# S loaded twice over on ScalarE's queue and turned by VectorE, in an attention and FFN kernel on one core

## The chip, the cores and the metric

The kernel runs on one core of a Trainium2 chip. The metric is the device time of one execution in microseconds (us), given as the median over several runs. The engines are TensorE (PE in the profile, with PEld for its weight loads), VectorE (DVE), ScalarE (ACT), GpSimd (POOL) and SyncE (SP); SP and ACT each have a queue on which they issue DMA transfers.

## The reference

Attention by a polynomial sketch, without a softmax, followed by a feed-forward layer (FFN) with a squared ReLU. There are 4 batches of 4 heads, 1088 positions and 32 dims per head; the sketches S1 and S2 are 8 x 32 each. The FFN has 4352 tokens, width 128 and 2048 hidden units.

```python
def phi(x):
    a = np.einsum('rd,bhsd->bhsr', S1, x)
    b = np.einsum('rd,bhsd->bhsr', S2, x)
    return np.einsum('bhsi,bhsj->bhsij', a, b).reshape(*x.shape[:-1], r * r)
q_p, k_p = (phi(q), phi(k))
kv = np.einsum('bhsf,bhsd->bhfd', k_p, v)
z = np.sum(k_p, axis=2)
num = np.einsum('bhsf,bhfd->bhsd', q_p, kv)
den = np.einsum('bhsf,bhf->bhs', q_p, z)[..., None] + 1e-06
x = ...      # num / den, heads side by side, 4352 x 128
h = np.maximum(x @ w_in, 0.0)
out = h * h @ w_out
```

## The kernel before

All of it is float32, with the first FFN matmul in a packed form of it. The tokens of the FFN are cut into ten chunks of 256 to 512 columns (`FC`). For each chunk and each of 16 blocks of 128 hidden units, TensorE multiplies `xT` by a block of `w_in` (L583, "pg"), ScalarE takes the ReLU (L592, "gt"), ScalarE or VectorE squares it (L600, L602, "g"), and TensorE multiplies by a block of `w_o` into an accumulator (L621, "po").

The attention of the batches is computed between those pieces. A planner, `_Order`, places them by costs and due times that are written into the code, and writes one fixed order for every engine. The change doesn't touch the planner's part. It touches the stretch before it, the first 14 us, where the order is the order of the program: the attention of batch 0, of which the first 256 queries are computed in one piece so that the FFN can start.

That stretch runs as follows. S1 is loaded by ACT's queue and S2 by SP's queue into `s_nat`, 8 rows each (L217, L218). On SP's queue there follow k of batch 0 in two parts, the first 256 columns of q, eight transfers of v, then in turn two quarters of `w_in`, a quarter of `w_o`, columns 256 to 640 of q, and the remaining weights. TensorE meanwhile runs five dummy matmuls (`keep_warm(W0)`, L672, 512 columns of bfloat16 ones, into "warm"). It then multiplies `s_nat` by a selection matrix `sel` (L683, four matmuls into "sp"). `sel` is built from an identity by VectorE's memset and two GpSimd copies (L230, L249, L252). ScalarE copies the result to `ss` (L686), 128 partitions by 80 columns: the first 64 columns, `sf`, hold the transposed S of each head in a block of its own, zeros elsewhere; the last 16, `s_T`, hold the transposed S1 and S2 in every head's 32 partitions. Four more dummies follow (`keep_warm(W1)`).

VectorE transposes k into `kt0` in three pieces (`a_kT0`, L283) and the first q into `qT` (L289). TensorE computes k's features, nine tiles of 128 positions (`a_kf`, L308, "kf", against `sf`), and ScalarE copies half of them to `kb` (L314). VectorE multiplies them to the 64 products `kp` (`a_kp0`, L324). TensorE sums them against v into "kvp" (`a_kv0`, L384). In between it computes both sketches of the first queries (`q0`, L734, tile "x", against `sq`, which GpSimd makes from `s_T` at L699). From "kvp" VectorE makes block matrices `bd` (L766) and `zm`, TensorE the denominator and numerator (L789), and VectorE the first 256 columns of `xT` (L812). With these the FFN starts (L583). `a_qc` (L296) computes the sketches of the second chunk of queries, from the transposed columns 256 to 640 of q.

On GpSimd the order is: memsets, the identity `iden`, the two `sel` copies, `sq`, then `irep` (four copies, L706), memsets, two copies of `s_T` into `sw` (L713), `sfk` (L714), memsets, and then the four casts of `w_in` (`cast_wi`, L665).

Of the kernel before, what the change touches and what calls it, by code (L numbers as in the profile page):

```python
# [9 lines left out]
F32 = mybir.dt.float32  # L10
# [4 lines left out]
def _ap(t: bass.AP, p0: int, np_: int, off: int, free):  # L15
    p = list(t.ap)[0]
    return bass.AP(
        t.tensor, t.offset + p0 * p[0] + off, [[p[0], np_]] + [list(d) for d in free]
    )
# [85 lines left out]
def kernel(  # L105
# [11 lines left out]
    nc = tc.nc  # L117

    B, H, S, D = 4, 4, 1088, 32
# [3 lines left out]
    E = 2  # L123
    NB = 16
    GT, G2, LA = 4, 6, 3.5
    LU = 4
    W0, W1, W3 = 5, 4, 1
    ND, QT, WI, KL, QL = 2, 3.0, (1.0, 1.9), (30.0, 12.0), 4.0


# [21 lines left out]
    psf = ctx.enter_context(tc.tile_pool(name="psf", bufs=2, space=bass.MemoryType.PSUM))  # L152
# [3 lines left out]
    def sb(name, cols, dt=F32, rows=128):  # L156
        return cpool.tile([rows, cols], dt, tag=name, name=name)
# [7 lines left out]
    kT, qT = sb("kT", SP), sb("qT", SP)  # L165
    xT = sb("xT", B * S + SP - S, F32R)
    w_in32, w_o, w_in = sb("w_in32", 2048), sb("w_o", 2048), sb("w_in", 2048, F32R)
    s_nat, ss, s2f = sb("s_nat", 32, rows=16), sb("ss", 80), sb("s2f", 32)
    sf, s_T = ss[:, 0:64], ss[:, 64:80]

    sw = [sb(f"sw{i}", 32) for i in range(2)]
    sfk = sb("sfk", 32)
# [3 lines left out]
    def load_k(eng, b, c0=0, c1=S):  # L176
        eng.dma_start(
            kn[b % 2][:, c0:c1],
            bass.AP(k.tensor, k.offset + b * H * S * D + c0, [[G * D, 128], [1, c1 - c0]]),
        )  # L180

    def load_q(eng, b, c0, c1):
        eng.dma_start(
            qn[b % 2][:, c0:c1],
            bass.AP(q.tensor, q.offset + b * H * S * D + c0, [[G * D, 128], [1, c1 - c0]]),
        )
# [16 lines left out]
    def load_wi(eng, c):  # L203
        eng.dma_start(
            w_in32[:, 512 * c : 512 * c + 512], moe_w_in[:, 512 * c : 512 * c + 512]
        )
# [7 lines left out]
            ),  # L214
        )

    nc.scalar.dma_start(s_nat[0:8, :], S1[:, :])  # L217
    nc.sync.dma_start(s_nat[8:16, :], S2[:, :])  # L218
    load_k(nc.sync, 0, 0, 512)
    load_k(nc.sync, 0, 512, S)  # L220
    load_q(nc.sync, 0, 0, 256)
# [4 lines left out]
    zero_a = sb("zero_a", 8)  # L226
    nc.scalar.copy(zero_a[:, :], nc.const_aps.tensor(0.0, (128, 8), F32))

    sq, sel = sb("sq", 256), sb("sel", 320, rows=16)
    nc.vector.memset(sel[:, :], 0.0)  # L230
    nc.gpsimd.memset(_ap(vn[0], 96, 32, 32 * (NT - 2), [[32 * NT, H], [1, 64]]), 0.0)
    nc.gpsimd.memset(vn[0][:, VC : VC + 32], 1.0)
    ones = vn[0][:, VC : VC + 32]
# [8 lines left out]
    for i in range(2):  # L242
        nc.vector.memset(own_p[64 * i : 64 * i + 64, i : i + 1], 1.0)
    iden, irep = sb("iden", 128), sb("irep", 128)
# [1 line left out]

    own_f, zm = sb("own_f", 16), sb("zm", 32)
    own_h, own_q = sb("own_h", 4), sb("own_q", 2)
    nc.gpsimd.tensor_copy(  # L249
        _ap(sel, 0, 16, 0, [[88, 4], [32, 2], [1, 8]]), _ap(iden, 0, 16, 0, [[0, 4], [8, 2], [1, 8]])  # L250
    )
    nc.gpsimd.tensor_copy(  # L252
        _ap(sel, 0, 16, 64, [[80, 4], [1, 16]]), _ap(iden, 0, 16, 0, [[0, 4], [1, 16]])
    )
    nc.vector.tensor_reduce(
        out=own_h[:, :], in_=_ap(iden, 0, 128, 0, [[32, 4], [1, 32]]), op=add, axis=AX
    )
# [22 lines left out]
    def a_kT0(t0, n):  # L280
        p = 3 if t0 + n > NT - 2 else 4
        i = 32 * (first(0, t0, 1) - first(0, t0, 0))
        nc.vector.transpose(  # L283
            _ap(kt0, 0, 128, 128 * t0, [[32, p], [128, n], [1, 32]]),
            _ap(kn[0], 0, 128, 32 * first(0, t0, 0), [[i, p], [32, n], [1, 32]]),
        )
# [16 lines left out]
    def a_kf(t0, n, pool, tag):  # L303
        kf = pool.tile([128, 512], F32, tag=tag, name="kf")
        for t in range(n):
            for c in range(4):
                o = 128 * (t0 + t) + 32 * c
                nc.tensor.matmul(  # L308
                    _ap(kf, 32 * c, 32, 32 * t, [[32 * n, 2], [1, 32]]),
                    kt0[:, o : o + 32],  # L310
                    sf,
                )
        kb = wpool.tile([128, 32 * 3], F32, tag="kb", bufs=4, name="kb")
        nc.scalar.copy(kb[:, 0 : 32 * n], kf[:, 32 * n : 64 * n])  # L314
        st["kf", t0] = kf, kb
# [137 lines left out]
    def a_w(b):  # L453
        pw = wpool.tile([128, 64], F32, tag="pw", bufs=1, name="pw")
        nc.vector.tensor_tensor(
            out=pw[:, :],
            in0=_ap(st[b, "kvp"], 0, 128, 32, [[64, E], [8, 4], [1, 8]]),
            in1=_ap(ss, 0, 128, 72, [[0, E], [0, 4], [1, 8]]),
            op=mult,
        )  # L460
        nc.vector.tensor_reduce(
            out=sw[b % 2][:, 16:24], in_=_ap(pw, 0, 128, 0, [[8, 8], [1, 8]]), op=add, axis=AX
        )
# [205 lines left out]
    def keep_warm(n, cols=512):  # L669
        t_ = st["warm"]  # L670
        for _ in range(n):
            nc.tensor.matmul(  # L672
                t_[:, 0:cols],
                nc.const_aps.tensor(1.0, (128, 128), mybir.dt.bfloat16),
                nc.const_aps.tensor(1.0, (128, cols), mybir.dt.bfloat16),
            )
# [1 line left out]

    st["warm"] = psf.tile([128, 512], F32, tag="pg", name="warm")
    keep_warm(W0)  # L680
    sp = psf.tile([128, 512], F32, tag="po", name="sp")
    for h in range(H):
        nc.tensor.matmul(  # L683
            sp[32 * h : 32 * h + 32, 0:80], s_nat[:, :], sel[:, 80 * h : 80 * h + 80]
        )
    nc.scalar.copy(ss[:, :], sp[:, 0:80])  # L686
    load_wi(nc.sync, 0)
    load_wi(nc.sync, 1)
    load_wo(nc.sync, 0)
# [3 lines left out]
    for c in range(1, 4):  # L693
        load_wo(nc.sync, c)
    load_q(nc.sync, 0, 640, S)
    keep_warm(W1)
    a_kT0(0, 4)
    for x in range(2):
        nc.gpsimd.tensor_tensor(  # L699
            out=_ap(sq, 0, 128, 128 * x, [[64, 2], [8, 8], [1, 8]]),  # L700
            in0=_ap(ss, 0, 128, 72 - 8 * x, [[0, 2]] + [[[0, 8], [1, 8]], [[1, 8], [0, 8]]][x]),
            in1=_ap(own_q, 0, 128, 0, [[1, 2], [0, 8], [0, 8]]),
            op=mult,
        )
    for h in range(H):
        nc.gpsimd.tensor_copy(  # L706
            _ap(irep, 32 * h, 32, 0, [[32, 4], [1, 32]]),
            _ap(iden, 32 * h, 32, 32 * h, [[0, 4], [1, 32]]),
        )
    nc.gpsimd.memset(_ap(vn[1], 96, 32, 32 * (NT - 2), [[32 * NT, H], [1, 64]]), 0.0)  # L710
    for w in sw:
        nc.gpsimd.memset(w[:, 16:32], 0.0)
        nc.gpsimd.tensor_copy(w[:, 0:16], s_T)  # L713
    nc.gpsimd.tensor_tensor(  # L714
        out=_ap(sfk, 0, 128, 0, [[16, 2], [1, 16]]),
        in0=_ap(ss, 0, 128, 64, [[0, 2], [1, 16]]),
        in1=_ap(own_q, 0, 128, 0, [[1, 2], [0, 16]]),
        op=mult,
    )
# [17 lines left out]
    qb0 = wpool.tile([128, 512], F32, tag="qb0", bufs=1, name="qb0")  # L737
    qp0 = wpool.tile([128, 512], F32, tag="qp0", bufs=1, name="qp0")
    a_kf(0, 2, psf, "po")
    a_kf(2, 2, psf, "pg")  # L740
    a_kf(4, 3, psf, "po")
    a_kf(7, 2, psf, "pg")
    q0(0)
# [3 lines left out]
    for t0, n in ((0, 2), (2, 2), (4, 3), (7, 2)):  # L747
# [5 lines left out]
        out=_ap(qp0, 0, 128, 0, [[256, 2], [1, 256]]), in0=banks(x0, 2, 0, 256),  # L753
        in1=_ap(qb0, 0, 128, 0, [[256, 2], [1, 256]]), op=mult,
    )
    nc.vector.transpose(s2f[:, :], _ap(ss, 0, 128, 72, [[0, 4], [1, 8]]))
    den0 = psf.tile([128, 512], F32, tag="po", name="den0")
    for y in range(2):
        nc.tensor.matmul(  # L759
# [13 lines left out]
    for c in range(4):  # L773
# [4 lines left out]
        in0=_ap(st[0, "kvp"], 0, 128, 32, [[64, 2], [0, 2], [1, 8]]),  # L778
        in1=_ap(own_f, 0, 128, 0, [[0, 2], [8, 2], [1, 8]]),
# [173 lines left out]
    def kv_tasks(b, k0):  # L953
        O.add(
            ("kvs", b), {"PE": 1.6}, k0, [("vn", b), ("ks", b, 3)], on(a_kvs, b),
            uses=[("kp", b, h) for h in range(H)], rings=[("att", 1)], lag=PEL,
        )
        O.add(
            ("w", b), {"DVE": 0.3}, k0 + 0.9, [], on(a_w, b), uses=[("kvs", b)],
        )  # L960
        O.add(
            ("kvt", b), {"DVE": 0.2}, k0 + 1.0, [("kvr", b - 1, 3)], on(a_kvt, b),
            uses=[("kvs", b)],
        )
        w = [("nd", b - 2, i) for i, _ in AC[b - 2]] if b > 1 else []
        for h in range(H):
            O.add(
                ("kvr", b, h), {"POOL": 0.95}, k0 + 2.0 + 0.1 * h, w + [("kvt", b)],
                on(a_kvr, b, h),
            )  # L970
# [21 lines left out]
    for u in range(NU):  # L992
        ci, c0, n, d0, m = units[u]
        w = n * m
# [37 lines left out]
        if d0 + m == NB and ci != last:  # L1032
            po = [x for u_ in range(first_unit[c0], u + 1) for x in pe2[u_]]
# [49 lines left out]
```

## Time and profile before

| | |
|---|---|
| median of 3 runs | 187.0 us (186.67, 187.0, 187.8) |
| the profiled execution | 187.0 us, of which the profile's span is 185.0 us |
| mean granted TensorE clock | 0.999 |
| PE busy | 180.1 us, 97% of the span |
| PEld busy | 104.4 us, 56% |
| ACT busy | 135.0 us, 73% |
| DVE busy | 120.1 us, 65% |
| POOL busy | 35.2 us, 19% |
| DMA | 11.25 MB, mean 61 GB/s |

The span runs from the first to the last instruction of the program; what lies around it is the difference to the execution's time. A busy time is the union of an engine's instructions, so that two that overlap count once. In a timeline line the first number is the start in us, the second the length of the merged group, then the engine, the line of the kernel, the operation, the tiles (written tile, arrow, read tiles) and the count; the bracket gives the idle time before the group and what ended it. A matmul on float32 stands as two records. DMA issues stand under SPq or ACTq, the time being that of the issue and not of the transfer.

### The profile page before, as it was taken

To read this page: it belongs to the slowest core of one execution; us is meant where nothing else is said; L and a number is where in the kernel's file an instruction comes from. 1 tells how busy PE (TensorE), PEld (TensorE's weight loads), DVE (VectorE), ACT (ScalarE), POOL (GpSimd) and SP (SyncE) were. 2 spreads that over 40 slices of the span, in tenths; PEclk is the share of its full clock that TensorE was granted. 3 is DMA by queue.
4 is the path that set the end of the run, shared out by engine and by line. 5 is a ranking of instruction groups with operands and counts; after the bars stand their busy time and mean duration, and the time that the engine had idled before them with its cause. 6 is when DMAs were issued, how large, how long until landed. Compare 5 with 4: busy or idle time off the path is not lost.

```text
span 185.0 us, 3893 instructions
## 1 busy us (share of the span) xinstructions
PE 180.1 (97%) x1478; PEld 104.4 (56%) x1478; DVE 120.1 (65%) x254; ACT 135.0 (73%) x262; POOL 35.2 (19%) x157
## 2 busy tenths in 40 slices
PE   8999999999999999999999999999999999999992
PEld 2757766666555566555454445545545555555791
DVE  4968969968994598699437984998243334222420
ACT  3319977769968887699585975795788878777760
POOL 4425405328400000870000003820000000000000
PEclk9999999999999999999999999999999999999999
DMA  4799700100038700000592100002103000300211
GB/s 160 186 334 330 177 4 2 25 7 4 0 50 226 181 0 0 4 0 10 92 310 40 21 0 5 0 4 39 20 0 57 0 0 8 52 0 0 31 25 28
DMA packets 24673, 11.25 MB, mean 61 GB/s; under 512 B 18000, under 2 KB 23120, under 8 KB 24656
## 3 DMA queue, kind: packets, MB, share of 16 engines
q1 hardware_dynamic: 24448, 10.95, 24.4%
q8 instruction: 11, 0.18, 0.5%
q10 hardware_dynamic: 208, 0.07, 0.2%
q14 instruction: 6, 0.05, 0.1%
HBM read 8.78 MB, written 2.23 MB: 60 GB/s over the span
## 4 chain that ended last, share of the span: by engine, by line
PE 97%; DVE 0%; issue 0%
PE po L621 60%; PE pg L583 18%; PE nd L536 4%; PE warm L672 2%; PE kvp L402 2%; PE pol L616 2%; PE po L616 2%; PE qc L296 2%; PE kvp L384 1%; PE kf L308 1%; PE kc L338 1%; PE x L734 1%; PE num L789 0%; PE den L789 0%; PE den L759 0%; PE x L427 0%
## 5 line engine op out<-in xcount | busy, mean ns | idle before, releaser
L621 PE MATMUL po<-g,w_o 128*128 128x512 f32 (+3 forms) x288 | 123.8, 548 | 0.0
L592 ACT ACTIVATE gt<-pg 128x512 f32<-128x512 f32 (+3 forms) x145 | 75.3, 569 | 33.8 <-PE pg L583 33.3
L621 PEld LDWEIGHTS po<-g,w_o 128*128 128x128 f32 x288 | 53.0, 189 | 32.4 <-issue 23.9
L583 PE MATMUL pg<-xT,w_in 128*128 128x512 f32 (+3 forms) x160 | 69.2, 516 | 0.6 <-DVE xT L812 0.4
L600 ACT ACTIVATE g<-gt 128x512 f32<-128x512 f32 (+2 forms) x105 | 60.0, 603 | 1.4
L602 DVE TENSOR_TENSOR g<-gt 128x512 f32<-128x512 f32 (+3 forms) x40 | 27.0, 678 | 40.8 <-ACT gt L592 40.2
L583 PEld LDWEIGHTS pg<-xT,w_in 128*128 128x128 f32 x160 | 29.0, 190 | 29.6 <-ACT gt L592 11.3
L443 POOL COPY kv<-kvt 32x64 f32<-32x64 f32 x48 | 12.1, 253 | 64.6 <-DVE kvt L420 62.5
L497 POOL COPY rd<-rc 32x9 f32<-32x9 f32 (+2 forms) x80 | 16.0, 200 | 13.5 <-DVE rc L489 10.1
L506 DVE STREAM_SHUFFLE qa<-qc 128x576 f32<-128x576 f32 (+2 forms) x20 | 11.6, 652 | 0.0
L521 DVE TENSOR_TENSOR qp<-qa,qb 128x576 f32<-128x576 f32 (+2 forms) x20 | 10.8, 604 | 0.0
L355 DVE TENSOR_TENSOR kp<-fs 128x576 f32<-128x576 f32 x12 | 8.4, 755 | 0.1
L469 DVE STREAM_TRANSPOSE qt<-qc 128x576 f32<-128x576 f32 (+2 forms) x10 | 5.8, 613 | 4.0 <-PE qc L296 4.0
L625 DVE STREAM_TRANSPOSE oT<-po 128x512 f32<-128x512 f32 (+3 forms) x9 | 5.9, 650 | 2.4 <-PE po L621 2.4
L536 PE MATMUL nd<-qp,kv 32*32 32x288 f32 (+2 forms) x320 | 6.8, 353 | 0.0
L553 DVE TENSOR_TENSOR xT<-nd,bc 128x576 fp32r<-128x576 f32 (+2 forms) x10 | 5.6, 599 | 1.0 <-PE nd L536 1.0
L289 DVE STREAM_TRANSPOSE qT<-qn 128x192 f32<-128x192 f32 (+3 forms) x11 | 5.9, 567 | 0.2 <-DMA qn<-in_q_dram 0.2
L506 DVE STREAM_SHUFFLE qb<-qc 128x576 f32<-128x576 f32 (+2 forms) x10 | 6.0, 651 | 0.0
L536 PEld LDWEIGHTS nd<-qp,kv 32*32 32x32 f32 x320 | 3.8, 103 | 3.7 <-issue 2.2
L546 DVE STREAM_TRANSPOSE bc<-rd 128x576 f32<-128x576 f32 (+2 forms) x10 | 5.7, 598 | 0.3 <-POOL rd L497 0.3
L616 PE MATMUL pol<-w_o,g 128*128 128x128 f32 x32 | 5.7, 275 | 0.0
L616 PE MATMUL po<-w_o,g 128*128 128x128 f32 x32 | 5.7, 275 | 0.0
(92 smaller groups left out, 89.6 us busy)
## 6 DMA issues: line engine op xcount, KB each, us to landing
kn<-in_k_dram SPq DMA_DIRECT2D x3, 544.0 KB, 5.6
qn<-in_q_dram SPq DMA_DIRECT2D x3, 544.0 KB, 6.1
vn<-in_v_dram SPq DMA_DIRECT2D x9, 144.0 KB, 4.4
w_in<-in_moe_w_in_dram SPq DMA_DIRECT2D x4, 256.0 KB, 5.5
w_o<-in_moe_w_out_dram SPq DMA_DIRECT2D x4, 256.0 KB, 5.5
out_dram<-oT SPq DMA_DIRECT2D x12, 64.0 KB, 2.0
out_dram<-oT SPq DMA_DIRECT2D x8, 56.0 KB, 2.0
out_dram<-oT SPq DMA_DIRECT2D x8, 48.0 KB, 1.9
```

Source lines behind the costliest of these rows:

```text
L355: nc.vector.tensor_tensor(out=_ap(st[b, "kp"], 0, 128, 64 * NT * h, [[64, NT], [8, 8], [1, 8]]), in0=_ap(fs, 0, 128, o, [[32, NT], [1, 8], ...
L443: nc.gpsimd.tensor_copy(_ap(st[b, "kv"], 32 * c, 32, 64 * h, [[32, E], [1, 32]]), _ap(st["kvt"], 32 * h, 32, 0, [[64, E], [1, 32]]),)
L497: nc.gpsimd.tensor_copy(st[b, "rd", i0][32 * h : 32 * h + 32, n * c : n * c + n], st["rc"][32 * c : 32 * c + 32, n * h : n * h + n],)
L506: nc.vector.stream_shuffle(in_=banks(st[b, "qc", i0], 2 * x, 0, m), out=_ap(st[b, which, i0], 0, 128, 2 * m * x, [[m, 2], [1, m]]), mask=m ...
L521: nc.vector.tensor_tensor(out=st[b, "qp", i0, e][:, r], in0=st[b, f"qa{e}", i0][:, r], in1=st[b, "qb", i0][:, r], op=mult,)
L536: nc.tensor.matmul(nd[32 * h : 32 * h + 32, 512 * c : 512 * c + m], kv[r, o : o + 32], qp[r, m * h : m * h + m], start=(e == 0), stop=(e = ...
L583: nc.tensor.matmul(st["pg", u][:, n * i : n * i + n], w_in[:, 128 * (d0 + i) : 128 * (d0 + i) + 128], xT[:, c0 : c0 + n],)
L592: nc.scalar.activation(gt[:, 0:w], st["pg", u][:, 0:w], Relu)
L600: nc.scalar.activation(g2[:, 0:w], gt[:, 0:w], Square)
L602: nc.vector.tensor_tensor(out=g2[:, 0:w], in0=gt[:, 0:w], in1=gt[:, 0:w], op=mult)
L616: nc.tensor.matmul(po[x // 128][:, 0:128], g[:, x : x + 128], w, start=(d == 0), stop=(d == NB - 1),)
L621: nc.tensor.matmul(po[0][:, 0:n], w, g, start=(d == 0), stop=(d == NB - 1))
```

## The change

S is no longer brought into place by TensorE. Both halves of S are loaded on ACT's queue, each row twice, so that `s_nat` has 32 rows; VectorE transposes this 32 x 32 block into `s_tt`. `sf` and `s_T` become tiles of their own. `sf` is set to zero by VectorE, and GpSimd (heads 3 and 1) and ScalarE (heads 2 and 0) copy the blocks into it; GpSimd copies `s_T`, four times. `sel`, its copies and the four matmuls on it are gone. SP's queue now begins with k. The five and four dummies become eight in a row, ahead of kf, and one dummy of 256 columns stands between the second and the third group of kf. GpSimd makes `irep` before these copies, not after `sq`. What read `ss` reads `s_T` or `sf`.

```diff
-    W0, W1, W3 = 5, 4, 1
+    W0, W3 = 8, 1
...
-    s_nat, ss, s2f = sb("s_nat", 32, rows=16), sb("ss", 80), sb("s2f", 32)
-    sf, s_T = ss[:, 0:64], ss[:, 64:80]
+    s_nat, s_tt, s2f = sb("s_nat", 32, rows=32), sb("s_tt", 32, rows=32), sb("s2f", 32)
+    sf, s_T = sb("sf", 64), sb("s_T", 16)
...
-    nc.scalar.dma_start(s_nat[0:8, :], S1[:, :])
-    nc.sync.dma_start(s_nat[8:16, :], S2[:, :])
+    def load_s(eng, x, src):
+        eng.dma_start(
+            s_nat[16 * x : 16 * x + 16, :], bass.AP(src.tensor, src.offset, [[D, 8], [0, 2], [1, D]])
+        )
+
+    load_s(nc.scalar, 0, S1)
+    load_s(nc.scalar, 1, S2)
...
-    sq, sel = sb("sq", 256), sb("sel", 320, rows=16)
-    nc.vector.memset(sel[:, :], 0.0)
+    sq = sb("sq", 256)
+    nc.vector.memset(sf[:, :], 0.0)
...
-    nc.gpsimd.tensor_copy(
-        _ap(sel, 0, 16, 0, [[88, 4], [32, 2], [1, 8]]), _ap(iden, 0, 16, 0, [[0, 4], [8, 2], [1, 8]])
-    )
-    nc.gpsimd.tensor_copy(
-        _ap(sel, 0, 16, 64, [[80, 4], [1, 16]]), _ap(iden, 0, 16, 0, [[0, 4], [1, 16]])
-    )
...
     keep_warm(W0)
-    sp = psf.tile([128, 512], F32, tag="po", name="sp")
     for h in range(H):
-        nc.tensor.matmul(
-            sp[32 * h : 32 * h + 32, 0:80], s_nat[:, :], sel[:, 80 * h : 80 * h + 80]
-        )
-    nc.scalar.copy(ss[:, :], sp[:, 0:80])
+        nc.gpsimd.tensor_copy(
+            _ap(irep, 32 * h, 32, 0, [[32, 4], [1, 32]]),
+            _ap(iden, 32 * h, 32, 32 * h, [[0, 4], [1, 32]]),
+        )
+    nc.vector.transpose(s_tt[:, :], s_nat[:, :])
+    for h, f in ((3, nc.gpsimd.tensor_copy), (2, nc.scalar.copy), (1, nc.gpsimd.tensor_copy),
+                 (0, nc.scalar.copy)):
+        f(_ap(sf, 32 * h, 32, 8 * h, [[32, 2], [1, 8]]), _ap(s_tt, 0, 32, 0, [[16, 2], [2, 8]]))
+    for h in range(H):
+        nc.gpsimd.tensor_copy(
+            _ap(s_T, 32 * h, 32, 0, [[8, 2], [1, 8]]), _ap(s_tt, 0, 32, 0, [[16, 2], [2, 8]])
+        )
...
-    keep_warm(W1)
     a_kT0(0, 4)
...
-    for h in range(H):
-        nc.gpsimd.tensor_copy(
-            _ap(irep, 32 * h, 32, 0, [[32, 4], [1, 32]]),
-            _ap(iden, 32 * h, 32, 32 * h, [[0, 4], [1, 32]]),
-        )
...
     a_kf(2, 2, psf, "pg")
+    keep_warm(1, 256)
     a_kf(4, 3, psf, "po")
```

More of the change, by code (lines that the diff above doesn't have):

```diff
@@ L310, in a_kf @@
                     kt0[:, o : o + 32],
-                    sf,
+                    sf[:, :],
                 )
@@ L457, in a_w @@
             in0=_ap(st[b, "kvp"], 0, 128, 32, [[64, E], [8, 4], [1, 8]]),
-            in1=_ap(ss, 0, 128, 72, [[0, E], [0, 4], [1, 8]]),
+            in1=_ap(s_T, 0, 128, 8, [[0, E], [0, 4], [1, 8]]),
             op=mult,
@@ L700 @@
             out=_ap(sq, 0, 128, 128 * x, [[64, 2], [8, 8], [1, 8]]),
-            in0=_ap(ss, 0, 128, 72 - 8 * x, [[0, 2]] + [[[0, 8], [1, 8]], [[1, 8], [0, 8]]][x]),
+            in0=_ap(s_T, 0, 128, 8 - 8 * x, [[0, 2]] + [[[0, 8], [1, 8]], [[1, 8], [0, 8]]][x]),
             in1=_ap(own_q, 0, 128, 0, [[1, 2], [0, 8], [0, 8]]),
             op=mult,
-        )
-    for h in range(H):
-        nc.gpsimd.tensor_copy(
-            _ap(irep, 32 * h, 32, 0, [[32, 4], [1, 32]]),
-            _ap(iden, 32 * h, 32, 32 * h, [[0, 4], [1, 32]]),
         )
@@ L712 @@
         nc.gpsimd.memset(w[:, 16:32], 0.0)
-        nc.gpsimd.tensor_copy(w[:, 0:16], s_T)
+        nc.gpsimd.tensor_copy(w[:, 0:16], s_T[:, :])
     nc.gpsimd.tensor_tensor(
         out=_ap(sfk, 0, 128, 0, [[16, 2], [1, 16]]),
-        in0=_ap(ss, 0, 128, 64, [[0, 2], [1, 16]]),
+        in0=_ap(s_T, 0, 128, 0, [[0, 2], [1, 16]]),
         in1=_ap(own_q, 0, 128, 0, [[1, 2], [0, 16]]),
@@ L755 @@
     )
-    nc.vector.transpose(s2f[:, :], _ap(ss, 0, 128, 72, [[0, 4], [1, 8]]))
+    nc.vector.transpose(s2f[:, :], _ap(s_T, 0, 128, 8, [[0, 4], [1, 8]]))
     den0 = psf.tile([128, 512], F32, tag="po", name="den0")
```

## The prediction

> **What bounds the kernel now.** I read the chain of waits first. It is TensorE (PE) almost alone.
>
> ```profile
> PE 97%; DVE 0%; issue 0%
> ```
>
> So time is gained only where PE starts a piece of its queue earlier, and the change touches nothing but the first 14 us. The same chain, cut to that stretch (start, length, piece):
>
> ```profile
> 0.77 2.29 PE warm L672 x5
> 3.06 0.42 PE sp L683 x8
> 3.48 1.82 PE warm L672 x4
> 5.30 2.07 PE kf L308 x72
> 7.37 1.06 PE x L734 x8
> 8.44 2.25 PE kvp L384 x72
> ```
>
> Nothing waits in it: dummies, the S matmuls, dummies again, k's features. Next, the timeline: what else was ready, and when.
>
> ```profile
> 1.17 0.83 SPq L177 DMA_DIRECT2D kn<-in_k_dram  x2
> 3.90 1.57 DVE L283 STREAM_TRANSPOSE kt<-kn 128x512 f32<-128x512 f32 x3 [1.36 <-DMA kn<-in_k_dram]
> 5.71 0.45 DVE L289 STREAM_TRANSPOSE qT<-qn 128x256 f32<-128x256 f32 x1 [0.24 <-DMA qn<-in_q_dram]
> 6.20 2.75 DVE L324 TENSOR_TENSOR kp<-kf,kb 128x512 f32<-128x512 f32 x4
> 7.76 0.50 SPq L183 DMA_DIRECT2D qn<-in_q_dram  x1
> 10.73 0.29 DVE L766 TENSOR_TENSOR bd<-kvp,own_p 128x128 f32<-128x128 f32 x1 [0.82 <-PE kvp L384]
> 13.51 0.63 DVE L289 STREAM_TRANSPOSE qT<-qn 128x192 f32<-128x192 f32 x2
> ```
>
> The first transposition of k (711 ns by the view of tile kt) ends at 4.61, yet kf starts at 5.23, behind the four dummies: they hold PE 0.6 us. The last line starts inside its predecessor (xT, 13.17 to 13.59) and shows no wait on its load. PE's own timeline shows what that qT feeds:
>
> ```profile
> 13.74 0.71 PE L583 MATMUL pg<-xT,w_in 128*128 128x256 f32 x4 [0.38 <-DVE xT L812]
> 14.38 0.45 PE L296 MATMUL qc<-qT,sw 32*32 32x96 f32 x32
> 14.94 0.47 PE L583 MATMUL pg<-xT,w_in 128*128 128x256 f32 x2
> ```
>
> Last, the list of DMA issues, for issue to landing of the neighbours of that q load:
>
> ```profile
> w_in<-in_moe_w_in_dram SPq DMA_DIRECT2D x4, 256.0 KB, 5.5
> w_o<-in_moe_w_out_dram SPq DMA_DIRECT2D x4, 256.0 KB, 5.5
> ```
>
> **SyncE's queue.** S2's issue leaves it, so k is issued at 0.74 in place of 1.17, and each load behind it 0.44 earlier. DMA share is 0.02 between 1 and 2 us, so nothing but the issue holds k. Bounds for the loads: 0 (the engines limit) to 0.44; I take 0.44, since the share is below 0.8 from 5 to 8 us, where v is issued in turn every 0.47 us. k lands at 3.46.
>
> **S by ScalarE's queue.** Its first issue is 0.73 to 1.32 (587 ns); the second ends at 1.7 to 1.9 (378 to 587 ns, the two S rows). In the landing records S1 was complete at 2.27, 1.54 after its issue; the first k load took 2.7. S2 lands at 2.9 at best and 4.0 at worst; I take 3.1, since its 1 KB is nearer to S1. [...] VectorE is free at 2.54 (own_f, 2.26 + 0.28), and turns S in 0.20 (the row of s2f): 3.3, ahead of k. Queued behind that wait stand kT, qT and kp, so an S later than 3.3 pushes all of them.
>
> **sf and s_T.** ScalarE's table load (1.28) and copy (0.20) slide behind the second issue, to about 3.4; two copies of some 0.2 (sw from x, 165 ns; kb, 212) end at 3.8. GpSimd loses two sel copies (0.4) and takes irep (1.32 for four) right after iden: 3.1. Then two sf copies (196 ns, the row of sw): 3.7; four s_T copies: 4.5; sq (0.76): 5.3, before 4.62. The rest (some 1.4) ends near 6.7; its next work, the casts, waits for w_in until 10.38 now, so that cover is wide. Without it each 0.1 would move the casts 0.1.
>
> **PE.** Eight dummies at 0.42 each ((2.29 - 0.63) / 4) from 0.77, and the 0.56 that kf stood behind the start of the last one (5.23 against 4.67): 4.28. kT's first piece is done at 3.46 + 0.71 = 4.17, sf at 3.8. So kf starts at 4.28, 0.95 earlier: the sp matmuls (0.42), one dummy (0.42) and their seams leave the path. kf takes 2.07 as now, plus the dummy of 256 columns (0.1 to 0.21): 6.5. q0 (1.06) has qT at 3.46 + (6.16 - 3.90) = 5.72 and sq at 5.3; end 7.6. kvp (2.25) ends at 9.9. It was 10.69.
>
> **The clock.** The PEclk row is full everywhere, but the rows show another step: a group of kf records (64 columns) takes (2.14 - 0.31) / 17 = 0.108 us, a pair of kvp records of the same 64 columns (2.32 - 0.22) / 35 = 0.060. PE went from half to full rate near 7.2. If the unbroken dummies bring that to 4.3, kf takes 1.0 and is done at 5.4; then VectorE rules: kp can start behind qT at 5.75, ends at 8.5, qp (0.69) and s2f (0.20) follow, and bd starts at 9.3 in place of 10.73, 1.45 earlier. If it stays at 7.2, bd comes at 9.95, 0.8 earlier. [...]
>
> **What is late next.** From bd to xT is a chain of 2.86 us, unchanged, so the first FFN matmuls could start 0.8 to 1.45 earlier, at 12.3 to 12.95; w_in's first cast (10.38 + 0.61 - 0.44) is done by then. But behind the first four of them PE has qc, which needs the q load issued at 7.76: by its neighbours' 5.5 it landed at 13.3, and at most at 13.5. Moved by 0.44 it lands at 12.9 to 13.05; the two qT take 0.63, the hop 0.1: qc at 13.65 to 13.8, against 14.38. That is 0.6 to 0.75, whatever the prologue gained beyond it. The FFN matmuls at 14.94, which follow qc, gain 0.75 (0.45 behind it), and the x of the second chunk, which the 384-column matmuls at 22.2 need, comes from VectorE's chain behind qc, so it moves as qc does. ScalarE, busy 4.00 of 4.00 us from 16 to 20, starts earlier by more than that, so it isn't late.
>
> **Sum.** 0.75 earlier from there on, and PE carries it to the end: span 185.0 - 0.75 = 184.25. The profiled execution took 187.0 with 2.0 around its span, and 187.0 is the median of the runs: 186.25, so 186.2.
>
> **Rivals.**
> A full gain: the q load is not what qc waits for. For it: page section 3 has 11 instruction packets with 0.5% of 16 engines' span, 1.35 us each on one engine, and one that falls elsewhere would let q land up to 1.3 earlier. Against: all the loads behind keep their order. Price: 1.3 to 1.45, so 185.6.
>
> The loads don't move: the engines and not the issue limit. For it: DMA share is 1.0 to 1.1 from 10 to 20 us. Against: 0.7 to 0.8 before. Then k lands at 3.90, kf starts at 4.7, and qc has only the slack that it had (qT ended at 14.14, qc started at 14.38): 0.15 to 0.25, so 186.8.
>
> [...]
>
> S held up: were it to land after 4.2, kT would end its first piece after 5.1 and kf start as late as before; the change would then do nothing of what it says. At my upper bound of 4.0 kT's first piece ends at 4.9, kf starts at 5.0 and everything on PE up to qc gains 0.2: 186.8.
>
> **How the numbers follow.** Chances: forecast 0.50, full gain 0.18, loads unmoved 0.12, late clock 0.12, S held up 0.08. The three runs of before lie from 186.67 to 187.8, so some 0.5 is noise on any of them. The range reaches from the full gain less 0.3 (185.3) to the loads unmoved, S held up and most of the late clock's lesser cases (187.5). One per cent, 1.87 us, is about what a measurement can tell from no change. Over 1% faster needs the full gain and luck: 0.09. Over 1% slower needs a gate missed for two windows: 0.07. Within: 0.84.
>
> **What would show it.** Right: kn issued at 0.74, kt transposed from about 3.46, kf from 4.28, bd between 9.3 and 10.0, the qT pair waiting on its load for 0.3 us or more and starting near 13.0, qc near 13.7 with a gap on PE ahead of it. Wrong: kf's groups at 0.108 and kvp's pairs at 0.12 (the late clock); kt waiting on s_tt; kn landing at 3.9; qc without a gap.

## The result and the profile after

| | before | after |
|---|---|---|
| median, us (runs; lowest to highest) | 186.84 (21; 186.15 to 189.45) | 189.29 (21; 187.2 to 190.43) |
| ratio to before, 95% interval | | 1.0104, 1.0082 to 1.0127 |
| profiled execution, us (its span) | 187.0 (185.0) | 188.74 (187.0) |

The change made the kernel about 1% slower, where 0.4% faster was forecast. The ratio leaves out the executions that took over 1.5% more than the fastest of their kernel (three of after, one of before). In the two profiled executions all of the loss arises ahead of the first FFN matmul. From there on the two profiled executions run the same order at a nearly constant distance: the first FFN matmul starts at 15.82 in place of 13.74, which is 2.08 later, and the span is 2.0 longer.

The page of after, first the granted clock in 40 slices of 4.7 us, then the chain that ended last by engine.

```profile
PEclk9789999999999999999999999999999999999999
...
PE 94%; DMA 2%; DVE 1%; ACTq 1%; issue 0%; DVEq 0%
```

The chain is no longer TensorE alone: a DMA and ACT's queue stand in it, 3% of the span together. The clock has a dent in the second and third slice, which the page of before does not show; but in the trace of before the first clock record starts at 7.24, the page shows the time ahead of it as full, and TensorE ran at half rate until then, as the prediction read from the rows (0.108 us for a group of kf, 0.060 for a pair of kvp). The chain itself, in order of time (start, length, piece), shows who:

```profile
0.74 1.30 ACTq L218
...
2.07 3.28 DMA s_nat<-in_S_dram
...
5.45 0.20 DVE s_tt L685
5.65 0.60 DVE kt L282
...
6.39 0.65 PE kf L307 x32
7.04 0.22 PE warm L671
7.26 1.23 PE kf L307 x40
8.48 2.01 PE x L734 x8
10.49 2.29 PE kvp L383 x72
```

In this stretch it begins with the load of S. By the landing records of the trace, S1 is there at 3.56 and S2 at 5.35; before, they were there at 2.27 and 2.09. The transposition of S waits for it, and that of k, whose data have been there since 3.48, stands behind that wait on VectorE. So kf starts at 6.39. Against the chain of before (kf 5.30, x 7.37, kvp 8.44) the loss adds up in two terms: kf starts 1.09 later, and x takes 2.01 in place of 1.07, 0.94 more. With 0.02 in kf and 0.04 in kvp that is 2.09.

The timeline of after (start, length, engine, line, what; the bracket is the idle time before, and what ended it):

```profile
0.74 0.87 SPq L177 DMA_DIRECT2D kn<-in_k_dram  x2
0.74 2.02 ACTq L218 DMA_DIRECT2D s_nat<-in_S_dram  x2
0.77 3.32 PE L671 MATMUL warm<-const-bfloat16-1.0 128*128 128x512 bf16 x8 [0.77 <-PEq L1068]
...
5.45 0.20 DVE L685 STREAM_TRANSPOSE s_tt<-s_nat 32x32 f32<-32x32 f32 x1 [3.00 <-DMA s_nat<-in_S_dram]
5.58 1.38 DVE L282 STREAM_TRANSPOSE kt<-kn 128x512 f32<-128x512 f32 x3
...
6.67 0.92 SPq L204 DMA_DIRECT2D w_in<-in_moe_w_in_dram  x2
...
8.11 0.51 SPq L183 DMA_DIRECT2D qn<-in_q_dram  x1
...
12.82 0.29 DVE L767 TENSOR_TENSOR bd<-kvp,own_p 128x128 f32<-128x128 f32 x1 [0.86 <-PE kvp L383]
```

k is issued at 0.74, as forecast; the two loads of S hold ACT's queue for 2.02, not for 0.96 (587 + 378 ns) as the two of before would have. VectorE sits idle for 3.00 ahead of s_tt. SP's queue does not keep its lead. Its issues of q and of the second transfer of v take 0.62 and 0.68 (0.43 in before), and its sixth transfer of v waits on the semaphore that counts S2's landing: it is issued at 5.36, where before it was at 4.90. So the first w_in load is issued at 6.67 and the second q load at 8.11, 0.34 and 0.35 later than in before (6.33 and 7.76), and not 0.44 earlier. The dummies end at 4.09, and PE has nothing until 6.39. What that gap does to the second term shows in the table by windows (PE, PEld, DVE, ACT, POOL as busy share and count; then the granted clock, the share of the DMA engines, GB/s):

```profile
4.00:5.00 1.00, 0.10 (x1) 0.00 (x0) 0.00 (x0) 0.26 (x2) 0.00 (x0) 1.00 0.79 209
5.00:6.00 1.00, 0.00 (x0) 0.00 (x0) 0.55 (x2) 0.31 (x2) 0.25 (x2) 1.00 0.68 181
6.00:7.00 1.00, 0.61 (x33) 0.55 (x33) 1.00 (x4) 0.22 (x2) 0.82 (x5) 1.00 0.57 142
7.00:8.00 1.00, 1.00 (x36) 0.88 (x37) 1.00 (x3) 0.30 (x2) 0.86 (x4) 0.56 0.61 119
8.00:9.00 1.00, 1.00 (x22) 0.75 (x16) 1.00 (x2) 0.45 (x2) 0.94 (x8) 0.50 0.96 214
9.00:10.00 1.00, 1.00 (x8) 0.67 (x4) 0.95 (x2) 0.00 (x0) 0.22 (x3) 0.50 0.72 202
```

PE is busy for 0.1 of the 2 us from 4 to 6, and the granted clock falls to one half just after, while kf's second part and x run. By the clock records of the trace the full rate is there from 3.71 to 7.12, one half from 7.12 to 10.54, and the full rate again from 10.54 to the end. So in this execution the full rate was there at 3.71 (before, it came at 7.24), and the gap behind the dummies lost it again for 3.41 us.

### The profile page after: what moved, and what is told of

Its sections match the earlier page's. It is cut to its first block, busy times and chain, and to the rows that moved or that the text cites. A ratio compares the mean times of both kernels' runs of the same rounds, so it can differ in the third digit from the quotient of the medians.

```text
span 187.0 us, 3878 instructions
## 1 busy us (share of the span) xinstructions
PE 179.5 (96%) x1469; PEld 104.6 (56%) x1470; DVE 119.3 (64%) x255; ACT 135.0 (72%) x263; POOL 35.9 (19%) x161
## 4 chain that ended last, share of the span: by engine, by line
PE 94%; DMA 2%; DVE 1%; ACTq 1%; issue 0%; DVEq 0%
PE po L620 60%; PE pg L582 18%; PE nd L535 3%; PE kvp L401 2%; PE pol L615 2%; PE po L615 2%; DMA s_nat<-in_S_dram 2%; PE qc L295 2%; PE kvp L383 1%; PE x L734 1%; PE kc L337 1%; PE kf L307 1%; ACTq L218 1%; PE den L790 0%; DVE kt L282 0%
```

## The experiments

The theory: S lands late, for two reasons (each row loaded twice makes the issue longer, and k's load is in flight beside it), and the gap that this tears into PE's work costs the clock. Rivals: the turning of S by VectorE costs by itself; the lower clock is chance and not the gap; the loads that now come earlier collide with something later. Ratios are to before, with 95% intervals; e3, e5, e7, e10 and e11 load each row of S once (8 rows, with the copies from `s_tt` adapted and the rest of `s_nat` set to zero by GpSimd, ahead of the loads). In the expectations "the gate" is shut while TensorE's granted clock is one half, and open at the full rate.

| run | median, us (n) | ratio | S turned | kf | x, us | first FFN matmul | span |
|---|---|---|---|---|---|---|---|
| after | 189.29 (21) | 1.0104, 1.0082 to 1.0127 | 5.45 | 6.39 | 2.08 | 15.82 | 187.0 |
| e1 | 188.61 (10) | 1.0065, 1.0032 to 1.0099 | 3.08 | 5.57 | 2.02 | 15.46 | 187.6 |
| e2 | 187.76 (7) | 1.0048, 1.0026 to 1.0069 | 5.13 | 6.07 | 1.13 | 14.00 | 186.0 |
| e3 | 187.86 (10) | 1.0023, 0.9983 to 1.0063 | 4.37 | 5.31 | 1.79 | 14.96 | 186.2 |
| e4 | 187.38 (10) | 1.0016, 0.9983 to 1.0049 | (before) | 4.77 | 1.18 | 13.33 | 185.4 |
| e5 | 187.38 (10) | 1.0019, 0.9985 to 1.0054 | 2.57 | 4.90 | 1.14 | 12.87 | 186.2 |
| e6 | 188.06 (8) | 1.0068, 1.0037 to 1.0100 | (before) | 6.51 | 1.13 | 15.03 | 186.2 |
| e7 | 186.83 (10) | 0.9991, 0.9961 to 1.0021 | 4.32 | 5.26 | 1.14 | 13.19 | 184.5 |
| e8 | 187.66 (10) | 1.0040, 1.0008 to 1.0071 | (before) | 4.74 | 2.08 | 14.53 | 185.7 |
| e9 | 190.83 (1) | | 4.25 | 8.23 | 1.81 | 17.90 | 189.0 |
| e10 | 187.30 (12) | 1.0035, 0.9998 to 1.0071 | 4.45 | 5.39 | 1.13 | 13.31 | 185.0 |
| e11 | 187.32 (10) | 1.0022, 0.9985 to 1.0060 | 2.54 | 4.76 | 1.14 | 12.83 | 185.4 |
| e12 | 186.24 (10) | 0.9985, 0.9950 to 1.0021 | (before) | 5.23 | 1.13 | 13.29 | 184.3 |

The last five columns are times in us of the one profiled execution, the medians and ratios those of all executions of a run; one execution can differ from the median by 0.3% and more. "S turned", "kf" and "first FFN matmul" are the starts, x is the length of that piece in the timeline. e9 was executed once.

**e1: S2 on SP's queue again, ahead of k.** From after:

```diff
-    load_s(nc.scalar, 1, S2)
+    load_s(nc.sync, 1, S2)
```

> The changed kernel with S2's load put back on SyncE's queue, ahead of k; all else as changed. Theory 'late S' (S2 is late because it is issued second on ScalarE's queue and shares the DMA engines with k and q; it landed at 5.35): S2 is issued at 0.74, s_tt starts by 2.9, kt at 3.9, kf at 4.7 where the changed kernel had 6.39, PE has no gap over 0.7 us ahead of kf and no half rate from 7.1 to 10.5; ratio to before 0.993 to 1.000. Theory 'doubled rows' (an issue with each row twice is slow in itself): S1's issue still takes 1.3 us and lands at 3.5; s_tt at 3.6; kf then at about 5.0. Theory 'the rest of the change costs' (copies of sf, GpSimd's order): ratio stays at 1.005 or above though S is early.

The timeline of e1:

```profile
0.73 0.84 SPq L218 DMA_DIRECT2D s_nat<-in_S_dram  x1
0.74 1.28 ACTq L218 DMA_DIRECT2D s_nat<-in_S_dram  x1
...
3.08 0.20 DVE L685 STREAM_TRANSPOSE s_tt<-s_nat 32x32 f32<-32x32 f32 x1 [0.64 <-DMA s_nat<-in_S_dram]
4.72 0.71 DVE L282 STREAM_TRANSPOSE kt<-kn 128x512 f32<-128x512 f32 x1 [1.44 <-DMA kn<-in_k_dram]
```

With S on both queues and ahead of k, S is turned at 3.08, 2.4 earlier than in after, so its place made S late: second on one queue, beside k. But k, issued behind a load of 0.84 us, now ends last: kt starts at 4.72, where before it started at 3.90. A row loaded twice costs on either queue: the issue took 1.28 on ACT's and 0.84 on SP's, 0.59 and 0.38 in before. Here the full rate came only at 9.98, so that x took 2.02, and PE paused later in the span as well (below, with e11). The ratio, 1.0065, is the one that the third theory gave, that the rest of the change costs; e5, where the rest stays and k comes in time, speaks against it.

**e2: fourteen dummies.** From after, to fill most of the gap and leave S as late as it is:

```diff
-    W0, W3 = 8, 1
+    W0, W3 = 14, 1
```

> The changed kernel with 14 dummies in place of 8 ahead of kf, so that TensorE stays busy to 5.2 (six more at 0.215 from 3.71 on). Theory 'shut clock' (the 2.3 us without matmuls, 4.1 to 6.4, bring the half rate from 7.1 to 10.5, and that is 1.5 of the 2.1 us lost by 12.8): kf starts at 6.4 as in the changed kernel, but its second part takes 0.65 in place of 1.29 and q0 1.1 in place of 2.1; bd at about 11.4 in place of 12.82; ratio 1.000 to 1.005. Theory 'late S alone': half rate or not, kvp cannot start before VectorE's kp, and the ratio stays near 1.010.

The timeline of e2:

```profile
6.87 0.77 PE L307 MATMUL kf<-sf,kt 128*32 128x64 f32 x40
7.57 1.13 PE L734 MATMUL x<-qT,sq 64*128 64x256 f32 x8
...
14.49 0.64 DVE L288 STREAM_TRANSPOSE qT<-qn 128x192 f32<-128x192 f32 x2 [0.63 <-DMA qn<-in_q_dram]
...
15.01 0.68 PE L295 MATMUL qc<-qT,sw 32*32 32x96 f32 x32 [0.30 <-DVE qT L288]
```

S is turned at 5.13, still late, but kf's second part takes 0.77 (1.29 in after) and x 1.13 (2.08): 0.52 and 0.95. With the 0.32 by which kf starts earlier here they make up nearly all of the 1.82 by which the first FFN matmul comes earlier (14.00). All that was added is work whose result nobody reads, and the intervals of the two ratios do not touch (1.0082 to 1.0127 against 1.0026 to 1.0069). So the gap costs the clock, and the clock some 1.5 us up to the first FFN matmul; at the end of the span 1.0 of the 1.82 is left (186.0 against 187.0), which is about what the ratios differ by. The last two lines show the wait that the prediction had named as the next one: the turned q waits 0.63 for its load, and qc for that.

**e3: each row of S loaded once.** From after, both loads still on ACT's queue:

```diff
-            s_nat[16 * x : 16 * x + 16, :], bass.AP(src.tensor, src.offset, [[D, 8], [0, 2], [1, D]])
+            s_nat[8 * x : 8 * x + 8, :], src[:, :]
...
+    nc.gpsimd.memset(s_nat[:, :], 0.0)
```

> The changed kernel with S loaded once (8 rows each, both still on ScalarE's queue; the block is set to zero by GpSimd first, and the copies take every column instead of every second). Theory 'doubled rows': the two issues take 0.6 and 0.4 in place of 1.30 and 0.68, S2 lands by 3.2, kf at 4.3 to 4.8, ratio below 1.000. Theory 'late S by sharing': the issues are hardly shorter, or S2 still lands after 4.5; kf after 5.6, ratio 1.003 to 1.010.

The timeline of e3:

```profile
0.88 0.90 ACTq L218 DMA_DIRECT2D s_nat<-in_S_dram  x2
...
4.37 0.20 DVE L686 STREAM_TRANSPOSE s_tt<-s_nat 32x32 f32<-32x32 f32 x1 [1.75 <-DMA s_nat<-in_S_dram]
```

The two issues take 0.90 (0.58 and 0.29) in place of 2.02, and S is turned 1.08 earlier. It is still 1.8 later than in e5, where S2 leaves on the other queue. S2 landed at 4.27, between what the two theories gave (3.2 and 4.5). The clock was late here too (full rate from 9.25), and the time fell to 1.0023 all the same.

**e4: the kernel before with two dummies fewer** asks what an earlier start of kf is worth when nothing else is touched.

```diff
-    W0, W1, W3 = 5, 4, 1
+    W0, W1, W3 = 5, 2, 1
```

> The kernel before with two dummies in place of four behind the S matmuls, nothing else. kt's first piece was ready at 4.61 and kf waited for the dummies until 5.23: kf should start at about 4.7. Theory 'PE's queue bounds the start': mm1 of the FFN starts 0.5 earlier and qc, held by the q load, 0.2 earlier: ratio 0.997 to 1.000. Theory 'clock first': two dummies fewer leave the gate shut longer than 7.2, kf and q0 at half rate, ratio 1.000 to 1.005.

kf started 0.46 and the first FFN matmul 0.41 earlier, and the time did not change measurably (1.0016). By the landing records k of batch 1 came at 22.98 (20.37 before); kc, which needs it, took 1.30 in place of 0.72, and the lead became 0.42 of lag.

**e5: S turned as in after, on the queues of before**, one row each: S1 on ACT's queue and S2 on SP's, ahead of k. From e3:

```diff
-    load_s(nc.scalar, 1, S2)
+    load_s(nc.sync, 1, S2)
```

> The changed kernel with S loaded once (8 rows each, the block zeroed first) and S2 on SyncE's queue ahead of k, S1 on ScalarE's: the turning by VectorE and the eight dummies without the move between queues and without the doubled rows. Theory 'late S': S lands by 2.4 as in the kernel before, s_tt at 2.6, kt at 3.9, kf at 4.7, the gap on PE is 0.4 and the gate never shuts; ratio 0.995 to 1.000. Rival 'the turning itself costs' (five small copies on two engines, GpSimd's later sq): kf still after 5.2, or q0 waits for sq; ratio 1.003 or more.

The timeline of e5:

```profile
2.57 0.20 DVE L686 STREAM_TRANSPOSE s_tt<-s_nat 32x32 f32<-32x32 f32 x1
4.04 1.54 DVE L283 STREAM_TRANSPOSE kt<-kn 128x512 f32<-128x512 f32 x3 [1.28 <-DMA kn<-in_k_dram]
...
9.87 0.29 DVE L768 TENSOR_TENSOR bd<-kvp,own_p 128x128 f32<-128x128 f32 x1 [0.60 <-PE kvp L384]
```

This is the prologue that was forecast: S turned at 2.57 without a wait, bd at 9.87, the first FFN matmul 0.87 earlier and qc at 13.51. So turning S on VectorE costs the prologue nothing. Yet the time was no better than before (1.0019, between the two forecasts). The list of PE's waits says why (who waited, for whom; total, times, longest):

```profile
PE pg L583 <- POOL w_in L665: 0.7, 1, 0.7
PE pg L583 <- DVE xT L553: 0.7, 1, 0.7
...
PE po L621 <- DMA w_o<-in_moe_w_out_dram: 0.2, 1, 0.2
```

PE was early and waited for the cast of a later quarter of w_in, for w_o, and for the next xT, which hangs on the q load that landed at 21.66 (17.96 before). None of these three waits is in the profile of before. Behind them stand late loads: SP's issue of the first quarter of w_o took 1.76 here (0.44 in before), so that the second q load was issued at 9.23 in place of 7.76 and the third quarter of w_in landed at 15.66 in place of 14.07. In before an issue as long (1.83, from 9.26) comes only behind those two.

**e6: the kernel before, with S2 moved to ACT's queue and nothing else.**

```diff
-    nc.sync.dma_start(s_nat[8:16, :], S2[:, :])
+    nc.scalar.dma_start(s_nat[8:16, :], S2[:, :])
```

> The kernel before with one edit: S2, 8 rows, issued on ScalarE's queue behind S1, so that SyncE's queue begins with k. Nothing doubled, nothing turned, nine dummies as before. Theory 'late S by sharing': S2 lands at about 4.2 in place of 2.1, the S matmuls start at 4.3 in place of 2.99, and with the four dummies behind them kf starts at 6.4 or later; ratio 1.003 to 1.012. Rival 'only the doubled rows are late': S2 lands by 3.0, kf starts at 5.2 as before, the loads come 0.4 earlier; ratio 0.996 to 1.000.

The timeline of e6:

```profile
3.44 1.52 DVE L283 STREAM_TRANSPOSE kt<-kn 128x512 f32<-128x512 f32 x3 [0.90 <-DMA kn<-in_k_dram]
...
4.27 0.49 PE L683 MATMUL sp<-sel,s_nat 16*32 16x80 f32 x8 [1.21 <-DVE kt L283]
```

k comes 0.46 earlier (3.44 against 3.90), and S2 lands at 4.14 in place of 2.09, so that the S matmuls start at 4.27, not at 2.99. The bracket names kt, whose first piece ended at 4.15; the S matmuls do not read it. Without VectorE's turning, without double rows and without the new dummies, this costs 0.68%.

**e7: e3 with eleven dummies.**

```diff
-    W0, W3 = 8, 1
+    W0, W3 = 11, 1
```

> The changed kernel with S loaded once on ScalarE's queue (as in the run with single rows) and 11 dummies in place of 8, so that TensorE is busy up to kf at 5.3. [...] Theory 'late S alone': the ratio stays at 1.002 or is higher, and the spread stays.

The gap ahead of kf is 0.6 in place of 2.3, the full rate is there from 3.51 and stays, x takes 1.14, and the time is that of before (0.9991), with the executions 1.2 us apart where those of e3 spread over 2.1. The single rows, and the dummies up to kf, take all of the 1% away.

**e8: the kernel before without its second dummies.** A gap of 1.26 in the old kernel, with S and k on time:

```diff
-    keep_warm(W1)
```

> The kernel before without the four dummies behind the S matmuls: S is on time, but TensorE idles from 3.5 to about 4.7. [...] Theory 'late S alone': nothing is late, the dummies were only in the way; ratio 0.996 to 1.000, spread as before.

kf starts at 4.74, half a microsecond earlier than before, and the full rate only comes at 9.58: x takes 2.08, and the time is 0.4% above before. The four dummies that held kf up were worth more than they cost.

**e9: k's load issued only after S is turned.** From after; a small copy of VectorE into `kn` makes the first k load wait for `s_tt`:

```diff
+    nc.vector.transpose(s_tt[:, :], s_nat[:, :])
+    nc.vector.tensor_copy(kn[0][0:32, 0:1], s_tt[:, 0:1])
```

> The changed kernel with one dependency added: the first k load waits until VectorE has turned S, so that S (each row twice, both on ScalarE's queue) has the DMA engines and the issuing hardware to itself. A measurement of S alone, slow as a whole since every load comes later. Theory 'late S by sharing': ScalarE's two issues get shorter than 1.30 and 0.68, the packets of S take less than 0.3 us in all, and s_tt starts at 3.2 or before, where it was 5.45. Theory 'doubled rows on one queue': the issues stay at 1.30 and 0.68, and s_tt starts at 3.7 or later though nothing else is in flight.

The timeline of e9:

```profile
0.73 2.02 ACTq L218 DMA_DIRECT2D s_nat<-in_S_dram  x2
...
4.25 0.20 DVE L224 STREAM_TRANSPOSE s_tt<-s_nat 32x32 f32<-32x32 f32 x1 [4.25 <-DMA s_nat<-in_S_dram]
```

It was run for one number. The issues take the same 2.02 with no load beside them, so their length is the double rows' own; S is turned 1.5 after the second issue's end (2.75), where with k in flight it took 2.7 (5.45). So 1.2 of S's delay is the company of the loads on SP's queue (k, q and the first of v), which all wait here, and the rest is the longer issue on one queue. Of the two theories the second had the issues and the start right (1.30 and 0.68, after 3.7); the first, by which the issues were to get shorter, had not, though the company costs too.

**e10: S2 on GpSimd's queue**, single rows, S1 on ACT's queue, k first on SP's, nine dummies:

```diff
-    load_s(nc.scalar, 1, S2)
+    load_s(nc.gpsimd, 1, S2)
...
-    W0, W3 = 8, 1
+    W0, W3 = 9, 1
```

> S loaded once, S1 issued by ScalarE and S2 by GpSimd's own queue, SyncE's queue begins with k, nine dummies: a try at both gains, S early and all loads 0.44 earlier. Theory 'late S by sharing': both halves still share the engines with k, S lands between 3.2 and 4.3, kf starts at 4.6 to 5.2, the gate does not shut; ratio 0.993 to 0.999. Rival: GpSimd's issue takes over 1 us ahead of iden and irep and its transfer is later than 4.3: kf after 5.3, ratio 1.000 to 1.006.

A third queue does not help: GpSimd issues from 1.27 to 1.97, and S is turned at 4.45, as on ACT's queue alone. The clock was early (4.24), the first FFN matmul 0.43 earlier than before, and the time not better (1.0035). S2 landed at 4.42 and kf started after 5.3, as the rival had it.

**e11 and e12: half of w_o not loaded**, from e5 and from before. They take 512 KB out of SP's queue behind the first quarters of the weights, to see whether those later loads are what eats e5's lead.

```diff
-    for c in range(1, 4):
-        load_wo(nc.sync, c)
+    load_wo(nc.sync, 1)
...
+    nc.gpsimd.memset(w_o[:, 1024:2048], 0.01)
```

> The kernel of e5 (S one row each, S1 on ACT's queue and S2 on SP's, turned by VectorE, eight dummies), with the last two quarters of w_o not loaded: 512 KB less on SP's queue, the hidden units 1024 to 2047 of w_o filled with a constant by GpSimd. So the output misses the true second half of the hidden units; PE's work is the same. Theory, the later loads bound the stretch from 16 to 26 us: k of batch 1 lands 1.5 to 2 earlier than in e5 (23.5), kT of batch 1 does not wait on it, and the FFN's start 0.87 earlier carries to the end: median 185.7 to 186.3, ratio 0.994 to 0.998, and 0.5 to 0.9 below e12. Rival, something else in the turned version costs it: no earlier than e12, ratio 1.000 to 1.003.

> The kernel before with the same 512 KB of w_o left out and filled by GpSimd (the output misses the true second half of the hidden units). Theory, the later loads bound the turned version but leave the kernel before some slack (its k of batch 1 landed at 20.37): median 186.6 to 187.0, ratio 0.998 to 1.001. Rival, the kernel before is held by the same loads: it gains as much as e11 does over e5, 0.5 or more.

e12 stayed at the time of before (0.9985), as its theory had it. In e11's profile the three waits of e5 are gone (k of batch 1 landed at 19.46, 23.47 in e5), and the lead over before holds from 0.91 at the first FFN matmul to 1.13 at the 17th (21.07 against 22.20). Then the timeline of e11 shows this:

```profile
22.97 0.70 PE L338 MATMUL kc<-kT,sfk 64*32 64x288 f32 x13
...
24.50 0.67 PE L338 MATMUL kc<-kT,sfk 64*32 64x288 f32 x3 [0.83 <-issue]
...
25.46 0.52 PE L583 MATMUL pg<-xT,w_in 128*128 128x384 f32 x1
```

Between the 13th and the 14th of the 16 records of kc, PE pauses for 0.83 with nothing that it waits for in the profile ("issue"). At the next FFN matmul the lead of 1.13 is a lag of 0.45, and so it stays. Such a pause stands in e1 too, where the lag grew from 1.50 to 2.52 at the same place. In both, the trace has a packet of 16 KB on the instruction queue (q8 in section 3 of the page) just ahead of it:

```
       packet (start, end)     last kc start before it    first after it   from packet's end
e1     23.78   25.20           25.91                      26.57            1.37
e11    21.70   23.16           23.27                      24.50            1.34
```

The other traces agree with this. In ten of the twelve the second packet of 16 KB ended more than 1.34 before kc, and kc shows no such pause (in e4 it is held by k); in e2 and e10 it ended 1.17 and 1.14 before it, and kc took 0.95 and 0.84 in place of 0.72. As a forecast of the time, the theory on the loads failed: 1.0022, where it gave at most 0.998, and inside what its rival gave. As a reading of the profile it held up to 22 us, and another pause took its place.

## Why the prediction was wrong

**The step that failed first** is the landing of S: "S2 lands at 2.9 at best and 4.0 at worst; I take 3.1". It landed at 5.35. Two terms were mis-sized. The issue: "the second ends at 1.7 to 1.9 (378 to 587 ns, the two S rows)" took the durations of 8 rows for loads that write 16; they were 1299 and 682 ns, and the second ended at 2.75, 0.85 later. The landing: the step took 1.2 from the issue's end (1.9 to 3.1) because "its 1 KB is nearer to S1", and with k in flight it was 2.60; in e9, with no load beside it, it was 1.39, so nearly all of this error is the company. So 3.1 + 0.85 + 1.4 = 5.35: the issue and the landing account for all of it. In before both S rows were issued ahead of any large load, so neither of them measured a small load in such company; the nearest row that did was the first k load itself, and the bound built on it, 2.1 from the end of the issue, was too short as well.

The move of S2 to ACT's queue saved 0.40 for k (3.88 to 3.48) and cost S 1.2 beside it (2.60 against the 1.39 of e9).

**The chance that was put too low** is that of the late clock, a half rate that lasts into x, 0.12. The step on the clock took two times for the full rate, 4.3 and 7.2, both with S at 3.1 and kf at 4.28. S at 5.35 gave PE a gap of 2.3, and the full rate of 3.71 was lost from 7.12 to 10.54: x took 2.01 in place of 1.07, and with the late start of kf beside it the time was 189.3. The late clock and "S held up" were counted as separate cases of 0.12 and 0.08, though in after the second brought the first about: with the gap mostly filled (e2), x took 1.13. "S held up" ended at the upper bound of 4.0, and so at a gain of 0.2 rather than a loss. The full gain fell outright. The loads that don't move came out half right, for a reason that it did not name: k moved (3.48), but from the third transfer of v on the loads were issued no earlier than before, and w_in and the second q load 0.34 and 0.35 later.

The 0.07 for over 1% slower ("a gate missed for two windows") and the upper end of the range, with "the late clock's lesser cases", were the author's estimate: no run shows such windows. What the runs showed is a stretch of half rate of 3.41 us in after, and a first full rate that came anywhere from 3.51 (e7) to 12.20 (e9). Ahead of that stretch the full rate had lasted from 3.71 to 7.12, with PE busy for 1.1 of the 3.41 us (3.71 to 4.09 and 6.39 to 7.12). The prediction asked only when the full rate would come, not whether it would last.

**What was right.** k was issued at 0.74 and landed at 3.48 (3.46 forecast); that "each load behind it" comes 0.44 earlier was not so in after, but was where S was loaded once and off SP's queue (e3, e6, e7, e10: w_in issued at 5.91 to 5.93 against 6.33). The full rate came early (3.71), but in e1 and e3, with the same eight dummies, only at 9.98 and 9.25: that was in part luck. The turning by VectorE takes 0.20, and with S on time (e5) bd came at 9.87, inside 9.3 to 9.95, and the first FFN matmul at 12.87, inside 12.3 to 12.95. The q load as the next wait is right in part: the transposition into qT waited for it 0.63 in e2, 0.36 in e10, 0.30 in e11 and 0.11 in e5 (landed at 14.46, 13.51, 12.96 and 12.81), and not in e7 (13.03); qc itself waited for it in e2 alone.

**A second step would have failed with S on time:** "0.75 earlier from there on, and PE carries it to the end". e5 came 0.87 earlier to the first FFN matmul, and e4 0.41, and neither was faster (1.0019, 1.0016; both intervals hold 1, and their lower ends lie at 0.998). The search for "what is late next" ended at qc. Behind it stand, in turn, the cast of w_in, w_o, the second q load, and k of batch 1. Even with 512 KB fewer of them a pause inside kc took what was left in the profiled execution of e11. That a lead is always lost is not shown: the profiled execution of e7 was 0.55 early at the first FFN matmul and ended 0.5 early (184.5), but e7's ratio shows no gain.

**What stays open.** Why k of batch 1 landed at 20.0 to 20.9 in some profiled executions (before, after, e3, e6, e7, e8, e10) and at 21.6 to 23.5 in others (e1, e2, e4, e5), with the same loads ahead of it (e9, e11 and e12 have others). One trace of it: in all 14 profiled executions an issue of 1.1 to 2.6 us on SP's queue, where 0.43 to 0.51 is usual, overlaps the first packet of 16 KB on the instruction queue (before: an issue of 1.83 from 9.26, the packet from 9.34), and that packet starts anywhere from 7.29 (e4) and 7.57 (e5) to 12.15 (e9). That the one holds up the other was not tested. That the pause in kc is PE waiting for its program is inferred from the times of packets; no edit tested it. And the profiled execution is one case of after: seven of its 21 executions have the mean clock of 0.991 that goes with this stretch of half rate, and nine have 1.0, so that in those the loss must stand elsewhere; in e1 and e3, whose mean clock is 1.0 as well, it stood in a full rate that came only during x.

## What to carry to other kernels

In this kernel a tiny load that everything waits for belongs ahead of the large ones, with each row loaded once; saving 0.4 us of another queue's issue was not worth its delay (e6 was 0.68% slower than before; e3's first FFN matmul came at 14.96, e5's at 12.87). Before a change that moves the first data of TensorE, ask what its queue holds until they come: the gap of 2.3 us at the start was paid twice here, once as time and once as clock, and dummies up to the last moment were the cheap insurance (e2, e7). And when a prologue becomes shorter, follow the loads for as many microseconds as they are issued ahead, not only to the next wait.

## What the runs showed of the hardware that was not expected

- The issue of a load from DRAM of 8 rows of 128 B took 569 to 587 ns as the first on ACT's queue and 288 to 378 ns as the second or on SP's queue (587 and 378 in before); with each row written twice, 1276 to 1299 ns and 682 to 844 ns (1299 and 682 in after), and the same with no other load in flight (1299 and 683 in e9).
- The second load of S, 2 KB, landed 1.39 us after the end of its issue with no other load in flight (e9), and 2.60 with those of k, q and v (after); the first landed 0.70 and 1.52 after. A third queue changed nothing (S turned at 4.45 in e10, 4.37 in e3).
- In after one PE gap of 2.3 us was followed by one stretch of 3.41 us at half the rate, which began 0.7 after PE was busy again; with a gap of 0.49 (e2) x took 1.13 in place of 2.08.
- TensorE paused for 0.26 (e1) and 0.83 us (e11) within a row of like matmuls with nothing that the profile shows to wait for; the next one started 1.37 and 1.34 after the end of an instruction packet of 16 KB that had come late (23.8 and 21.7, where in before the packet came at 17.8).
- A load's issue waited for another load through a shared semaphore: in after the sixth transfer of v was issued at 5.36, S2 having landed at 5.35, and in e2 at 5.05, S2 having landed at 5.03.
